# Delta-rule attention, then hash-routed experts, on one core: raw query products copied by ScalarE, the first expert's last rows computed with its early ones, weight loads and banks laid out anew

## The chip, the cores and the metric

One core of a Trainium2 chip runs the kernel in one launch. Its engines are TensorE (PE in the profile; PEld are its weight loads), VectorE (DVE), ScalarE (ACT), GpSimd (POOL) and SyncE (SP), whose queue issues most transfers. Each engine runs its instructions in order and waits on semaphores. The metric is the device time of one execution in microseconds (us). All data are float32.

## The reference

The first half is a delta-rule recurrence over 768 steps, for 4 batches of 8 heads with 48 numbers each; the second sends each of the 3072 resulting rows (384 wide) through one of 8 experts, chosen by a hash of its token number.

```python
for t in range(S):                       # S = 768
    y[:, :, t] = einsum('bhd,bhde->bhe', q_t, state)
    v_old = einsum('bhde,bhd->bhe', state, k_t)
    state = state + b_t * einsum('bhd,bhe->bhde', k_t, v_t - v_old)
...
expert_idx = token_ids * 2654435761 % 8
for e in range(8):
    xe = x[expert_idx == e]
    out[expert_idx == e] = maximum(xe @ w1[e], 0) @ w2[e]   # 384 -> 1024 -> 384
```

Here `k_t` is the normalised key, and `x` the attention's rows in the order of batch and step.

## The kernel before, in words

*Attention.* The 768 steps are 24 chunks of 32 (`c`), in groups of four (`g`). Partitions hold the four batches as quarters of 32. For each group keys and queries are loaded (`load_turn`) and turned by PE transposes and ACT copies into `KQ` (`turn`; L439, L444). Groups 2 and 3 keep theirs in the two `wide` tiles, which later hold the first expert's weights. `gram` (L465) forms products of keys with keys (`GK`, copied by ACT, L475) and of queries with keys (`GQ`). The latter are read from a PSUM bank by DVE and multiplied by a causal mask on the way (L481), with the highest priority. `inverse` (L553 to L596) inverts a 32x32 triangle for each head and chunk of a group by 31 pairs of DVE steps: a product into `tmp` (L596), a sum into `U` (L594). `turn_back` transposes it (L610). ACT spreads the result and the masked products over two halves (`Tz`, `MT`; L522).

`chunk(c)` is the recurrence: PE asks the state for keys and queries (L631), solves with `Tz` (L681), ACT copies `W` (L696), PE updates the state in `psS` (L704), ACT copies the new state (L727), PE adds the part inside the chunk (L744), ACT writes the rows to `x_sb` (L753), and GpSimd scatters them by expert to a buffer in HBM (L759). From chunk 20 on a chunk is split in halves. `scale_v` (L541) prepares V.

*The order.* Every piece of the attention is a `task` with an engine, an estimated time, names it reads and writes, and for PE a count of instruction words. `order` places the tasks on the engines by a list schedule with these estimates and the resulting order is emitted. It also models PE's code: blocks of 256 words, each `FETCH` = 3750 ns after the one before at the earliest. Idle PE time is filled with matmuls on an identity (L1124).

*Banks.* There are eight PSUM banks: two `z`, `psX`, `psY` and four slices of the tile `psS`, which serve as scratch (`homes`) until the first state update claims them.

*First expert.* `first_expert` loads the weights of the expert with rank 0 (`FIRST`) into the `wide` tiles once their keys are used up (L93, L959), in bursts of four transfers. When 18 of the 24 chunks are stored (`SOON`) it fetches 256 of its rows into `xq0` (the buffer's end is padded with zeros from `xq0` before, L969), and computes both layers for them (L995, L1006) after the last chunk. While the last inverse's memory becomes free, the second expert's weights are loaded by `parts`, three transfers at a chunk's store.

*Experts.* After the attention its PSUM pools close and new ones open (`ps_h` with 4 banks, `ps_t` and `ps_o` with 2 each). The loop over `RANKS` starts with `FIRST`, whose last up to 128 rows (the late column) are fetched into `xq_late` and go through `gemm1` (L1158) and `gemm2` (L1174). Each later expert has `gemm1`, whose evictions alternate between ACT (L1161) and DVE (L1163), then `gemm2_turned` (L1195) or `gemm2`. Between the hidden blocks of one expert, `between` loads weights and rows for those that follow and lets DVE turn the next one's rows (`turn`, L107). Rows go out by a GpSimd scatter (L1184). `xqs` are two row buffers, used in turn by rank.

Of the kernel before, what the change touches and what calls it, by code (L numbers as in the profile page):

```python
# [11 lines left out]
F32 = mybir.dt.float32  # L12
# [8 lines left out]
def kernel(  # L21
# [11 lines left out]
    nc = tc.nc  # L33
# [37 lines left out]
    xqs = [keep.tile([P, NBL, QW], F32, name=f"xq{i}") for i in range(2)]  # L71
    xq_late = keep.tile([P, P // C, QW], F32, name="xq_late")

# [67 lines left out]
    idx_i = keep.tile([P, SC], I32)  # L141
    numbers_first = wide[1][:, FO * DIN + SC * DIN:FO * DIN + SC * DIN + SC]
# [12 lines left out]
    with ExitStack() as phase1:  # L155
# [17 lines left out]
        ps = phase1.enter_context(tc.tile_pool(name="ps", bufs=1, space=PSUM))  # L173
# [35 lines left out]
        psS = ps.tile([P, B, BANK], F32, name="psS")  # L209
        homes = zs + [psX, psY] + [psS[:, b] for b in range(B)]  # L210
# [59 lines left out]
        def order():  # L270
# [27 lines left out]
            BLOCK, FETCH = 256, 3750.0  # L298
# [39 lines left out]
            while len(done) < n:  # L338
# [25 lines left out]
                if t["words"]:  # L364

                    for m in range(issued // BLOCK, (issued + t["words"]) // BLOCK + 1):
                        if m == len(begun):
                            if m > 1:
                                have = max(have, begun[-1]) + FETCH
                            begun.append(max(s, have))  # L370
                        s = max(s, begun[m])
# [78 lines left out]
        def gram(c, parts=(0, 1)):  # L450
# [21 lines left out]
            for r in range(2):  # L472
                if 0 in parts:
# [3 lines left out]
                             ACT.Copy), job=(job, r))  # L477
            for r in range(2):
# [165 lines left out]
        def chunk(c):  # L644
# [47 lines left out]
            over = ((len(zs), *range(len(zs) + 2, len(homes))), (1,)) if c == NU - 1 else ((), ())  # L692
            for i, hs in enumerate(hheads if split else (range(0, H),)):
                task("ACT", 300 if split else 390, (xn[i],),
                     (w_names[i],) if split else w_names,
                     lambda i=i, hs=hs: nc.scalar.activation(  # L696
                         W[:, hs.start:hs.stop], pws[i][:, hs.start:hs.stop], ACT.Copy),
                     release=over[i])
            if c < NU - 1:
                S1, K4 = Ss[(c + 1) % 2], K4s[c % 3]  # L700

                def update(us):
                    for u, b in pairs(us):
                        nc.tensor.matmul(  # L704
                            psS[:, b, 2 * D * u:2 * D * u + 2 * D],
# [10 lines left out]
                new = psS[:, :, 0:H * D].rearrange("p b (u r d) -> p b u r d", r=2, d=D)  # L716
                for i in range(2):
                    part = slice(HU // 2 * i, HU // 2 * i + HU // 2)
                    for r in range(2):

                        for q in range(2 if split else 1):
                            bs = slice(2 * q, 2 * q + 2) if split else slice(0, B)

                            def renew(r=r, q=q, bs=bs, part=part):
                                put, get = [t[half(r), bs, part, r] for t in (S1, new)]
# [221 lines left out]
        def first_expert():  # L947

            def weights(i):
                def go():  # L950
                    if not i:
                        which_first.append(expert_at(FIRST, mybir.EngineType.SP))
                        for part in w1_parts(which_first[0], w1_first, nc.sync):
                            part()
                        return
                    src = moe_w2[bass.ds(which_first[0], 1)].rearrange(
                        "o (f p) d -> p (o f) d", p=P)
                    for at in range(0, FO, 2):
                        nc.sync.dma_start(out=w2_first[:, at:at + 2], in_=src[:, at:at + 2])  # L959

                task("SP", 2500, ("lim",), tuple(
                    f"KQ{2 + i}{a}{b}" for a in range(2) for b in range(B)) + (f"w{1 + i}",), go,
                    kb=600)

            which_first = []
            weights(0)
            weights(1)
            rows = x_dram[N:].rearrange("n x -> (n x)").rearrange("(p y) -> p y", p=P)
            task("SP", 500, ("xq0",), ("x_pad",), lambda: nc.sync.dma_start(  # L969
                out=rows, in_=xqs[0].rearrange("p i x -> p (i x)")), kb=700, hold=120000)  # L970

            def early_rows():
                row = value(AT_ROW + E + 1, mybir.EngineType.SP, N)
                got = load_x(row, SC * P // C, xqs[0], nc.sync)
                got.append(load_numbers(row, SC, P, numbers_first[:, :, None], nc.sync))
# [345 lines left out]
```

## Time and profile before

| | |
|---|---|
| time, median of 9 runs | 524.84 us (520.92 to 529.6) |
| profiled execution, its own time | 520.77 us |
| its span | 519.2 us |
| granted PE clock over the span | 0.966 |
| PE busy | 469.7 us (90%), 6652 matmuls |
| DVE busy | 230.9 us (44%) |
| ACT busy | 189.3 us (36%) |
| moved by DMA | 60.61 MB, 117 GB/s over the span |
| DMA queue of instructions (q8) | 53 packets, 0.87 MB |

The span runs from the first to the last instruction that the profile shows; what lies around it, 1.6 us, is in the time of the execution. Shares of busy time are means over stages with different limits: attention fills the first 246 us, the first expert follows up to 279.16 us, and the seven others up to the last matmuls near 508 us. A line of a timeline gives start, duration, engine, line, operation, what it writes and reads, and how many instructions are merged; brackets give idle time of the engine before it and what ended it ("issue" is a wait for nothing that the profile shows).

| stage (us) | PE busy | DVE busy | ACT busy | clock | GB/s |
|---|---|---|---|---|---|
| 39 to 52 | 6.68 | 8.79 | 4.97 | 0.76 | 139 |
| 65 to 78 | 12.09 | 12.11 | 10.79 | 1.00 | 104 |
| 156 to 169 | 10.42 | 8.10 | 8.62 | 0.87 | 121 |
| 221 to 234 | 9.61 | 6.00 | 2.79 | 0.74 | 244 |
| 260 to 273 | 11.56 | 1.83 | 2.47 | 1.00 | 257 |

### The profile page before, as it was taken

What the parts mean: (1) busy time and instruction counts of PE and PEld (TensorE: products, weight loads), DVE (VectorE), ACT (ScalarE), POOL (GpSimd) and SP (SyncE); (2) the same over time, 40 slices, a digit from 0 to 9 for tenths busy, and PEclk for the clock granted to TensorE, in tenths of its full rate; (3) what the DMA queues carried; (4) which work ended last, traced back from release to release, by engine and by line L of the source; (5) the groups of instructions that cost most, each with busy time, mean ns of one, the idle gap of its engine ahead of it and who ended that gap; (6) DMA issues with size and microseconds to landing.
All of it is one profiled execution on the core that took longest, in us unless ns stands there. A gap on an engine that the chain in (4) does not pass through costs nothing. (4 is left out here: it accounts for less than half of the span.)

```text
span 519.2 us, 15841 instructions
## 1 busy us (share of the span) xinstructions
PE 469.7 (90%) x6652; PEld 318.7 (61%) x6652; DVE 230.9 (44%) x736; ACT 189.3 (36%) x415; POOL 70.5 (14%) x106
## 2 busy tenths in 40 slices
PE   8865999999998889879989999999999999999990
PEld 6654667777775667667766555556555565665650
DVE  5796899899896899643011202103012020120100
ACT  4633687888786687523120101101011010110100
POOL 6000011202101121111010001303102012102010
PEclk9977799999998999979999999999999999999997
DMA  9969757674567274591399954544943006401000
GB/s 142 167 101 139 135 103 140 131 136 89 145 138 125 53 202 96 127 242 53 85 257 197 239 113 131 121 91 136 190 144 82 0 24 160 150 0 42 2 29 15
DMA packets 136748, 60.61 MB, mean 117 GB/s; under 512 B 122957, under 2 KB 131265, under 8 KB 136676
## 3 DMA queue, kind: packets, MB, share of 16 engines
q1 hardware_dynamic: 131140, 49.80, 48.0%
q0 software_dynamic: 5344, 9.66, 5.8%
q8 instruction: 53, 0.87, 0.8%
q10 hardware_dynamic: 192, 0.12, 0.1%
q14 instruction: 19, 0.16, 0.1%
HBM read 49.19 MB, written 10.42 MB: 115 GB/s over the span
## 5 line engine op out<-in xcount | busy, mean ns | idle before, releaser
L1158 PE MATMUL h_ps<-xT,w_sb 128*128 128x424 f32 (+3 forms) x336 | 113.4, 491 | 0.0
L1158 PEld LDWEIGHTS h_ps<-xT,w_sb 128*128 128x128 f32 x336 | 62.9, 190 | 43.1 <-issue 14.9
L1163 DVE TENSOR_SCALAR h_sb<-h_ps 128x424 f32<-128x424 f32 (+4 forms) x32 | 17.0, 531 | 138.8 <-PE h_ps L1158 102.9
L1195 PE MATMUL oT_ps<-h_sb,w_sb 128*128 128x424 f32 (+1 forms) x192 | 66.4, 506 | 0.0
L596 DVE TENSOR_TENSOR tmp<-U,Ni 128x112 f32<-128x112 f32 (+15 forms) x186 | 61.6, 338 | 2.8 <-ACT U L580 0.2
L594 DVE TENSOR_TENSOR U<-U,tmp 128x112 f32<-128x112 f32 (+15 forms) x186 | 61.6, 338 | 2.9
L1184 POOL DMA_INDIRECT out_dram<-o_sb,tokens x26 | 30.3, 1167 | 208.0 <-ACT o_sb L1180 163.0
L1195 PEld LDWEIGHTS oT_ps<-h_sb,w_sb 128*128 128x128 f32 x192 | 36.2, 190 | 28.4 <-issue 15.6
L759 POOL DMA_INDIRECT x_scratch<-x_sb,slot x24 | 24.3, 1012 | 206.2 <-ACT MT L522 115.9
L727 ACT ACTIVATE S<-psS 48x384 f32<-48x384 f32 (+1 forms) x92 | 42.7, 464 | 14.3 <-PE psS L704 13.0
L1174 PE MATMUL o_ps<-w_sb,h_sb 128*121 128x384 f32 (+1 forms) x144 | 46.9, 486 | 0.0
L1161 ACT ACTIVATE h_sb<-h_ps 128x424 f32<-128x424 f32 (+4 forms) x32 | 15.0, 469 | 72.5 <-PE h_ps L1158 72.5
L1174 PEld LDWEIGHTS o_ps<-w_sb,h_sb 128*121 128x121 f32 (+1 forms) x144 | 26.6, 185 | 19.4
L744 PEld LDWEIGHTS psY<-W,MT 64*64 64x64 f32 x768 | 25.8, 139 | 14.2 <-issue 12.6
L704 PE MATMUL psS<-W,K 32*128 32x96 f32 x736 | 28.0, 281 | 6.2 <-ACT W L696 5.2
L1180 ACT COPY o_sb<-o_ps 106x384 f32<-106x384 f32 (+4 forms) x15 | 7.2, 479 | 69.5 <-PE o_ps L1174 55.1
L744 PE MATMUL psY<-W,MT 64*64 64x48 f32 x768 | 29.5, 225 | 3.1 <-issue 3.0
L681 PE MATMUL psX<-R,Tz 64*64 64x48 f32 x672 | 27.5, 223 | 3.4 <-issue 2.4
L704 PEld LDWEIGHTS psS<-W,K 32*128 32x128 f32 x736 | 23.7, 186 | 10.4 <-ACT W L696 7.7
L1197 ACT COPY oT<-oT_ps 128x424 f32<-128x424 f32 (+1 forms) x8 | 4.0, 499 | 70.9 <-PE oT_ps L1195 70.9
L681 PEld LDWEIGHTS psX<-R,Tz 64*64 64x64 f32 x672 | 23.4, 136 | 8.2 <-issue 4.7
L522 ACT ACTIVATE Tz<-TU,kmask 128x256 f32<-128x256 f32 x40 | 25.0, 720 | 0.5 <-DVE TU L610 0.5
(192 smaller groups left out, 583.8 us busy)
## 6 DMA issues: line engine op xcount, KB each, us to landing
w_sb<-in_moe_w_dram SPq DMA_DIRECT2D x32, 384.0 KB
w_sb<-in_moe_w_dram SPq DMA_DIRECT2D x6, 1536.0 KB
keys<-in_k_dram SPq DMA_DIRECT2D x24, 192.0 KB
Qt<-in_q_dram SPq DMA_DIRECT2D x24, 192.0 KB
V<-in_v_dram SPq DMA_DIRECT2D x96, 48.0 KB
K<-in_k_dram SPq DMA_DIRECT2D x96, 48.0 KB
wide<-in_moe_w_dram SPq DMA_DIRECT2D x8, 384.0 KB
xq<-x_scratch SPq DMA_DIRECT2D x12, 144.0 KB
```

The source lines that it names most:

```text
L522: lambda e=e: nc.scalar.activation(out[:, :, e].rearrange(order_of), in_.rearrange(order_of), ACT.Copy, scale=kmask[:, e:e + 1]))
L594: nc.vector.tensor_tensor(U[:, n:, 0:n], U[:, n:, 0:n], t, op=ALU.add)
L596: nc.vector.tensor_tensor(t, U[:, j:n, 0:n].to_broadcast([P, m, n]), Ni[:, j, n:, None].to_broadcast([P, m, n]), op=ALU.mult)
L681: nc.tensor.matmul(pws[i][rows, h], lhsT=Tz[rows, h].rearrange("p e i -> p (e i)"), rhs=R[rows, h], start=(h == (hs.start if split else 0) ...
L704: nc.tensor.matmul(psS[:, b, 2 * D * u:2 * D * u + 2 * D], lhsT=K4[quarter(b), u].rearrange("p r d -> p (r d)"), rhs=W[quarter(b), 2 * u:2 ...
L727: copy = nc.scalar.activation(put, get, ACT.Copy)
L744: nc.tensor.matmul(py[rows, h], lhsT=MT[rows, h].rearrange("p e i -> p (e i)"), rhs=W[rows, h], start=(c == 0 and h == 0), stop=True, skip ...
L759: put = nc.gpsimd.indirect_dma_start(out=x_dram[0:N, :], out_offset=bass.IndirectOffsetOnAxis(ap=slot[:, c:c + 1], axis=0), in_=x_sb, in_o ...
L1158: nc.tensor.matmul(h_ps[:, :width], lhsT=w1_sb[:, co, fo * P:(fo + 1) * P], rhs=xT[:, co, :width], start=(co == 0), stop=(co == CO - 1))
L1174: nc.tensor.matmul(o_ps[0:rows], lhsT=h_sb[:, fo, col * rows:(col + 1) * rows], rhs=w2_sb[:, fo, :], start=(fo == 0), stop=(fo == FO - 1))
L1184: scat = nc.gpsimd.indirect_dma_start(out=out[:, :], out_offset=bass.IndirectOffsetOnAxis(ap=idx, axis=0), in_=rows, in_offset=None, bound ...
L1195: nc.tensor.matmul(oT_ps[:, 0:width], lhsT=w2_sb[:, fo, i * P:(i + 1) * P], rhs=h_sb[:, fo, 0:width], start=(fo == 0), stop=(fo == FO - 1))
```

## The change

For chunks 0 to 11 the query products are copied raw from PSUM by ACT, and one DVE multiply in SBUF masks both halves, without the priority. The planner's model of code fetches gets two values, 4600 ns before 58 us and 3800 after. The four banks of `psS` are separate tiles until chunk 0's update, one tile while the state lives there, and separate again after the last `W`; the experts use the same eight banks (`hidden`, `results`) in place of pools of their own. The late column becomes a second set of tasks beside the first expert's early ones, with `xq0` and a new tile `late` as its buffers. The first expert's weights are eight single transfers, each tied in the plan to the store of a chunk from 11 to 18; the zeros are four transfers at chunks 5 to 8. The second expert's weights, the third's and the third's rows are issued after the second's rows, and the loop over experts leaves out `FIRST`. The second row buffer `xq1` lies in memory that opens after the attention.

```diff
-    xqs = [keep.tile([P, NBL, QW], F32, name=f"xq{i}") for i in range(2)]
+    xqs = [keep.tile([P, NBL, QW], F32, name="xq0")]
+    late = keep.tile([P, DIN], F32, name="late")
...
-        psS = ps.tile([P, B, BANK], F32, name="psS")
-        homes = zs + [psX, psY] + [psS[:, b] for b in range(B)]
+        others = ctx.enter_context(ExitStack())
+        homes = zs + [psX, psY]
+        state = []
+        def open_banks(in_one):
+            others.close()
+            pool = others.enter_context(tc.tile_pool(name="others", bufs=1, space=PSUM))
+            if in_one:
+                state[:] = [pool.tile([P, B, BANK], F32, name="psS")]
+            else:
+                homes[4:] = [pool.tile([P, BANK], F32, name=f"bank{i}") for i in range(B)]
+        open_banks(False)
...
-            BLOCK, FETCH = 256, 3750.0
+            BLOCK, FETCH, BUSY_FETCH, BUSY = 256, 3800.0, 4600.0, 58000.0
...
-                                have = max(have, begun[-1]) + FETCH
+                                have = max(have, begun[-1])
+                                have += BUSY_FETCH if have < BUSY else FETCH
...
+            if c < 3 * GC:
+                for r in range(2):
+                    task("ACT", 320, (names[r],), (f"GQ{c % 12}{r}",),
+                         lambda r=r: nc.scalar.activation(GQ[:, :, r], view(r)[:, :, 1],
+                                                          ACT.Copy), job=(job, r))
+                both = (f"GQ{c % 12}0", f"GQ{c % 12}1")
+                task("DVE", 340, both, both, lambda: nc.vector.tensor_tensor(
+                    GQ, GQ, mask[:, None, None, :].to_broadcast([P, HU, 2, C]), op=ALU.mult))
+                return
...
                 def update(us):
+                    if c == 0 and us.start == 0:
+                        open_banks(True)
...
-                task("SP", 2500, ("lim",), tuple(
+                task("SP", 600, ("lim", f"x_dram{11 + 4 * i + j}"), tuple(
                     f"KQ{2 + i}{a}{b}" for a in range(2) for b in range(B)) + (f"w{1 + i}",), go,
-                    kb=600)
+                    kb=380)
...
+            for i in range(4):
+                part = slice(NBL * QW // 4 * i, NBL * QW // 4 * (i + 1))
+                task("SP", 500, ("xq0", f"x_dram{5 + i}"), ("x_pad",), lambda part=part:
+                     nc.sync.dma_start(out=pad[:, part], in_=zeros[:, part]), kb=180)
...
+            columns("late", AT_ROW + E, slice(SC, SC + 1), NU, xq_late, "xq_late", xT_late)
+            for fo in range(FO):
+                job = new_job(1, early=True)
+                for co in range(CO):
+                    task("PE", 240, ("w1", f"xTlate{co}"), (f"j{job}",),
+                         lambda fo=fo, co=co, job=job: nc.tensor.matmul(
+                             bank(job)[:, 0:P], lhsT=w1_first[:, co, fo * P:(fo + 1) * P],
+                             rhs=xT_late[:, co], start=(co == 0), stop=(co == CO - 1)),
+                         words=2, job=(job, 0), idle=True, boost=-1e5)
...
-                if i in stores and parts:
-                    for part in parts[:3]:
-                        part()
-                    parts = parts[3:]
-            for part in parts:
-                part()
-            w_tiles[0] = w1_first, w2_first
...
+        xqs.append(m_q.tile([P, NBL, QW], F32, name="xq1"))
+        def hidden():
+            return homes[next(banks[0]) % 4]
+        def results():
+            return homes[4 + next(banks[1]) % 4]
...
-            fetch(FIRST)
             fetch(RANKS[1])
+            for part in parts:
+                part()
+            w_tiles[2] = load_w(expert_at(RANKS[2], mybir.EngineType.SP), w_pool2, nc.sync)
+            fetch(RANKS[2])
             n_ov = nc.values_load(ov_i[0:1, NOV:NOV + 1], min_val=0, max_val=NOV)
             for c in range(CO):
-                turn(FIRST, c)
+                turn(RANKS[1], c)
             for k in range(SC):
                 send_rows(o_first[:, k], idx_i[:, k:k + 1], True)
+            send_rows(o_late, idx_i[:, SC:SC + 1], True)
             for i, e in enumerate(RANKS):
+                if e == FIRST:
+                    continue
...
-                    to = i + 2 if i < 2 else i + 1
+                    to = max(3, i + 1)
```

`columns` is the fetch of rows, the DVE turns and the token numbers as they were in `first_expert`, for a given set of columns:

```python
def columns(name, at, ks, chunks, xq, xq_name, xT):
    n = ks.stop - ks.start
    task("SP", 2500, ("x_pad", "lim", *(f"x_dram{i}" for i in range(chunks))),
         (xq_name, "numbers" + name),
         lambda: rows_of(at, n, xq, numbers_first[:, ks]), kb=200 * n)
    for c in range(CO):
        task("DVE", 70 + 130 * n, (xq_name,), (f"xT{name}{c}",),
             lambda c=c: turn_x(xq, n * P // C, xT, c))
    task("DVE", 220, ("numbers" + name, "lim"), ("idx" + name,), lambda: number_of(ks))
```

## The prediction

> **What bounds the kernel now.** I read the page's slices first, then the timelines of TensorE (PE), VectorE (DVE) and the SyncE queue (SP). The slices (13 us each) show three stages:
>
> ```profile
> PE   8865999999998889879989999999999999999990
> DVE  5796899899896899643011202103012020120100
> PEclk9977799999998999979999999999999999999997
> ```
>
> The reader is to see that PE is full from the 20th slice on (the experts, from 246 us, at full clock) and has holes before it; that DVE is fullest in slices 3 to 16; and that the granted clock sinks in the 3rd to 5th slice, the 13th and the 18th. The change leaves the matmuls of the seven later experts as they are, so 279.16 us to the end (519.2) is taken as fixed. Three places before that are open.
>
> First, the time before chunk 0. Its solve needs the inverse of group 0, a chain of 62 dependent DVE steps (L594, L596) and a transpose (L610):
>
> ```profile
> 46.57 0.33 DVE L784 TENSOR_TENSOR rt<-rt,rt 128x176 f32<-128x176 f32 x1
> 49.98 0.29 DVE L481 TENSOR_TENSOR GQ<-psS,mask 128x128 f32<-128x128 f32 x1 [3.08 <-ACT GK L475]
> 50.72 0.29 DVE L481 TENSOR_TENSOR GQ<-psS,mask 128x128 f32<-128x128 f32 x1 [0.45 <-ACT GK L475]
> ...
> 52.85 0.36 DVE L594 TENSOR_TENSOR U<-U,tmp 128x207 f32<-128x207 f32 x1
> ...
> 60.50 0.51 DVE L481 TENSOR_TENSOR GQ<-z,mask 128x128 f32<-128x128 f32 x2 [1.33 <-ACT GK L475]
> 60.92 1.24 DVE L610 STREAM_TRANSPOSE TU<-U 128x1024 f32<-128x1024 f32 x1
> ```
>
> Columns: start, duration, engine, line, operation, and in brackets DVE's idle time and who ended it. The steps of U stand still from 46.8 to 52.85 us while DVE, in order, waits for products of queries (L481). Those products are needed by later chunks, not by this inverse. What they in turn waited for is PE's code:
>
> ```profile
> 49.04 0.34 PE L465 MATMUL psS<-wide 48*32 48x64 f32 x6 [4.04 <-issue]
> ...
> 63.57 1.14 PE L681 MATMUL psX<-V,Tz 64*64 64x48 f32 x32 [0.31 <-ACT Tz L522]
> ```
>
> At 49.04 PE had waited 4.04 us for nothing but "issue". Between that stop and the one before it (ended at 31.81) PE ran 383 matmuls and 383 weight loads, 766 instructions, three of the planner's blocks of 256:
>
> ```profile
> 31.00:48.50 17.50, 10.37 (x383) 9.48 (x383) 14.26 (x49) 6.71 (x17) 0.00 (x0) 0.77 0.81 112
> 62.50:161.00 98.50, 90.17 (x2486) 69.84 (x2486) 88.76 (x303) 81.37 (x178) 15.33 (x24) 1.00 0.64 128
> ```
>
> So an "issue" stop is a block of code that is late: three came in 17.2 us, 5.7 us each or less. From chunk 0 to chunk 12 PE takes one block in 5.07 us (4972 instructions in 98.5 us) and has 8.3 us idle.
>
> Second, the bursts of expert weights on SP, with the stops that follow:
>
> ```profile
> 149.03 3.13 SPq L93 DMA_DIRECT2D wide<-in_moe_w_dram  x4
> ...
> 216.47 1.35 SPq L93 DMA_DIRECT2D w_sb<-in_moe_w_dram  x3
> ```
> ```profile
> 161.81 0.30 PE L465 MATMUL z<-KQ 48*32 48x64 f32 x4 [2.58 <-issue]
> ...
> 226.27 1.51 PE L744 MATMUL psY<-W,MT 64*64 64x48 f32 x23 [3.02 <-issue]
> ...
> 265.37 2.20 PE L1006 MATMUL psS<-wide,keys 128*128 128x384 f32 x6 [0.47 <-ACT keys L1000]
> 268.54 5.62 PE L1158 MATMUL h_ps<-xT,wide 128*128 128x128 f32 x48 [0.96 <-ACT wide L1011]
> 274.00 5.33 PE L1174 MATMUL o_ps<-wide,h_sb 128*128 128x384 f32 x16
> 279.16 6.21 PE L1158 MATMUL h_ps<-xT,w_sb 128*128 128x424 f32 x17
> ```
>
> A stop of 2.58 us at 161.81 and one of 3.02 at 226.27 begin 10 and 7 us after bursts of 384 KB pieces (the first line group, from SP's queue; four at 149, eight from 216), and the clock then is 0.83 (161 to 171 us) and 0.84 (225 to 246). The last lines are the third place: the first expert's early columns end with a hole of 0.47, its late column begins after one of 0.96, and the next expert follows at 279.16.
>
> **The change, part by part.**
> *Raw products.* Summing the spells of L481 with their waits on DVE up to 60.92 us (18.6 to 19.24, 20.4 to 22.0, 24.8 to 25.5, 26.8 to 27.2, 33.2 to 35.4, 36.7 to 37.7, 46.8 to 52.85, 59.1 to 60.92): 0.6+1.6+0.7+0.4+2.2+1.0+6.1+1.8 = 14.4 us. In the built order of the changed kernel no L481 stands before the first L610 row; six masks do (the new multiply, 128x256 in SBUF, not shown here; the nearest row is L594 at 128x256, 425 ns): 6 x 0.43 = 2.5. Gain 11.9 at most. At least: 26 issue slots of 0.21 less 2.5, 3.0, if the waits only change place. PE's code is the next limit: before chunk 0's solve it has 2280 instructions instead of 2608 (counted in the built order: 2 for a transpose, 4 for a product), so block 9 is the last it needs; that block came at 49.04 already, and 51.7 us (63.57 less 11.9) is later. The 24 raw copies on ScalarE (ACT; nearest row L475, 411 ns) are 10 us at most; ACT is busy 5.7, 8.6, 4.9 and 5.0 of 13 us in the first four slices and hides them. Two new waits: MT spreads (L522) on ACT wait for DVE's mask, with transposed keys and PE behind them; the masks come early in DVE's order, so I take 0.9 off. I take **-11**.
>
> *Work put after chunk 0.* The built order has 32 transposes (8 groups of 4 at 0.58) and 64 products (60 records in 1.07 us, two records each: 2.3) more between the first solve and the last answer: 4.6 + 2.3 = 6.9 us of PE. Without such work a chunk takes 6.81 us (194.90 to 201.71); chunks 1 to 15 took 122.4, which is 20.2 over 15 x 6.81. Of that 5.5 are issue stops of 0.25 us or more, and 14.7 stand against 60 transposes and 320 products by the same rates, 8.7 + 11.4 = 20.1: 0.73. So 0.73 x 6.9 = **+5.0** (0 if the 8.3 us of holes take it, 6.9 if none).
>
> *Banks reopened at chunk 0.* The update of chunk 0 (L704) now waits until the four banks are read; in ACT's order two spreads (L522 Tz, 720 ns, 0.45 apart) and four raw copies (0.2 apart) stand between W and that: **+1.5** (0 to 2).
>
> *Weights.* The 1.5 MB bursts become eight 384 KB pieces, one a chunk, from chunk 11 to 18, and the second expert's 3.1 MB moves behind its rows, under the first expert. What the bursts cost: two chunks at 162 us took 21.5 against 18.2 by the rates above (6.81 each, 16 transposes 2.3, 64 products 2.3), 3.3; chunk 20 to 21 took 11.15 against 7.3 for the next, 3.9; together 7.2. The pieces still meet the code, so I take **-5** (0 to -7.2). On SP each piece stands ahead of one chunk's loads of K and V (0.45 us of issue; those loads are for two and four chunks later, which hides it). The 700 KB of zeros (134.60) go in four at chunks 5 to 8; no stop followed them, 0.
>
> [...]
>
> *Late column.* The same 32 matmuls, now mixed into the early ones: the two holes go (-1.4), one L995 of 0.43 comes back: **-1**. In the built order its first product stands 18 early and 8 output products behind the last answer, 13 us after it (18 x 0.43 + 8 x 0.65); its rows were turned 8 us after it (254 against 246), so it waits for nothing.
>
> *SP's new order.* Second expert's rows, its weights, the third's weights, the third's rows: 7.5 MB from 253.7. At the 257 GB/s of the slice from 260 that is 29 us: weights of the second by 269, needed at 278; third's rows at about 283. On DVE the turn of those rows (L107) stands after the eviction of the second hidden block, near 282.5, and the odd evictions (L1163) queue behind it; PE needs the first of their banks at 278 + 7 x 2.14 = 293 (evictions 4.27 us apart for two). Cover of 10 us, cost 0; gone, each us of lateness costs one.
>
> Sum: -11 + 5 + 1.5 - 5 - 1 = **-10.5**. The profiled execution took 520.77 (span 519.2 and 1.6 around it), so 510.3. It lies 4.1 under the median of the runs shown (524.84); against that median the forecast is **514**.
>
> **Rivals.**
> *No gain in sum* (the change doesn't do what it says). The planner puts masks and copies where its model has a block in 3.8 or 4.6 us; if blocks come at up to 5.7, DVE stands at masks as it stood at L481. With the least gain, -3 + 5 + 1.5 - 5 - 1 = -2.5: 522.3. For it: DVE still waits in order. Against: the masks wait on ACT alone, and six waits replace 26.
> *Slower: every piece meets a block.* Eight pieces instead of three bursts, while PE needs a block in 5.07 us. Without the burst term the sum is -5.5; if each piece costs 2.58, the smallest of the two stops, 20.6 less the 7.2 that go = +13.4, so +7.9: 532.7. It decides from (7.2 + 5.5 + 2.6)/8 = 1.9 us a piece. For it: the code's share is as tight as said. Against: the 1.5 MB issued from 185.40 to 188.94 caused no stop over 1 us.
> *More gain.* The holes take the moved work and the bursts' cost goes whole: -11 + 0 + 0 - 7.2 - 1 = -19.2: 505.6.
>
> **How the numbers follow.** Forecast 0.66, more gain 0.14, no gain 0.11, every piece 0.09. The range, 503 to 524, holds the first two with the bounds (-11.9 - 7.2 - 1.4 = -20.5, 504.3) and most of the third; above it lies the last rival. 0.5% (2.6 us) is about what a measurement here tells from no change: of the no-gain case 0.02 falls to faster and 0.01 to slower: faster 0.82, same 0.08, slower 0.10.
>
> **What would show it.** In the new profile: the first L610 transpose near 50 us and chunk 0's solve near 52; no DVE wait over 1 us at the masks; chunk 0 to chunk 4 about 3 us longer than the 29.9 of before; no issue stop over 2 us between chunk 11 and the end of attention, with a clock near 1.0 there; from the last answer to the second expert's first matmul 32 us (33.1 before). I am wrong if chunk 0's solve is after 58 us, if weights still stop PE, or if PE stands still in the second expert.

## The result and the profile after

The changed kernel takes 509.12 us (median of 20 runs, 504.5 to 516.35) beside 523.73 for the kernel before (62 runs): ratio 0.973, 95% interval 0.971 to 0.975. Ratios here and below leave out executions more than 1.5% above the fastest of their kernel, so they differ a little from the quotients of the medians. The forecast was 514 us with a range of 503 to 524. The profiled execution after took 509.12 us with a span of 507.5, where the one before took 520.77 with 519.2: 11.65 us less, where the prediction's sum said 10.5.

The page's slices of the changed kernel (12.7 us each):

```profile
PE   8974999999799798999999999999999999999990
DVE  5799899998897888571200203013021021110100
PEclk9977899999999999799999999999999999999996
```

From the 17th slice to the last but one PE shows nothing below 9; before, the last 8 stood in the 21st (which the prediction's "full from the 20th slice on" passed over). The granted clock still sinks at the start and once more, in the 17th slice; the sinks of the 13th and the 18th are gone.

VectorE's timeline of the changed kernel ahead of chunk 0 (start, duration, engine, line, operation; L503 is the new mask, L622 and L624 are the old L594 and L596, L638 the old L610):

```profile
41.68 0.37 DVE L624 TENSOR_TENSOR tmp<-U,Ni 128x207 f32<-128x207 f32 x1
41.97 0.42 DVE L503 TENSOR_TENSOR GQ<-GQ,mask 128x256 f32<-128x256 f32 x1
42.31 0.37 DVE L622 TENSOR_TENSOR U<-U,tmp 128x207 f32<-128x207 f32 x1
...
48.53 0.30 DVE L624 TENSOR_TENSOR tmp<-U,Ni 128x135 f32<-128x135 f32 x1
48.74 1.24 DVE L638 STREAM_TRANSPOSE TU<-U 128x1024 f32<-128x1024 f32 x1
```

TensorE's timeline just after it, with the idle time before a row and who ended it in brackets (L709 is the solve, L1192 a fill that keeps PE busy, L690 puts the next chunk's V into its bank, L779 is the answer, L738 the update):

```profile
51.32 1.94 PE L709 MATMUL psX<-V,Tz 64*64 64x48 f32 x32 [5.59 <-ACT Tz L550]
53.19 2.06 PE L1192 MATMUL psY<-ident 128*128 128x512 f32 x2
55.05 0.84 PE L690 MATMUL psX<-V,minus 128*128 128x384 f32 x2
55.82 1.14 PE L779 MATMUL psY<-W,MT 64*64 64x48 f32 x32
56.89 1.15 PE L738 MATMUL psS<-W,K 32*128 32x96 f32 x32
```

The mask stands in the chain of U like any other step, with no wait of its own, and the transpose comes at 48.74 us instead of 60.92. Chunk 0's solve follows at 51.32, 12.25 us earlier. But PE had then been idle for 5.59 us, the solve takes 1.94 us instead of 1.14 (the granted clock is 0.50 from 46 to 54 us), and the update of the state comes 5.57 us after the solve instead of 2.15.

From such rows the two profiled executions can be laid side by side, place by place:

| us | before | after | difference | the terms that met there |
|---|---|---|---|---|
| start to chunk 0's solve | 63.57 | 51.32 | -12.25 | raw products -11 |
| solve to update of chunk 0 | 2.15 | 5.57 | +3.42 | banks +1.5 |
| update of chunk 0 to that of 4 | 29.92 | 30.08 | +0.16 | moved work +3 (of the 5) |
| 4 to 12 | 66.41 | 66.82 | +0.41 | moved work, weights |
| 12 to 20 | 58.78 | 62.16 | +3.38 | moved work, weights |
| 20 to the last answer's end | 25.25 | 19.39 | -5.86 | weights |
| to the second expert's first matmul | 33.08 | 31.24 | -1.84 | late column -1 |
| to the end | 240.04 | 240.92 | +0.88 | SP's order 0 |

Between solve and last answer the sum is +1.51, and the prediction's three terms there gave 5 + 1.5 - 5 = 1.5. So the account by places came out nearly as forecast. Whether each gain belongs to the part of the change that was named for it is another question, and such a table can't answer it. The experiments answer it for most parts, and the answer is different.

### The profile page after: what moved, and what is told of

Its sections match the earlier page's. It is cut to its first block, busy times and chain, and to the rows that moved or that the text cites. A ratio compares the mean times of both kernels' runs of the same rounds, so it can differ in the third digit from the quotient of the medians.

```text
span 507.5 us, 15828 instructions
## 1 busy us (share of the span) xinstructions
PE 466.4 (92%) x6648; PEld 317.4 (63%) x6648; DVE 229.9 (45%) x720; ACT 191.9 (38%) x443; POOL 71.2 (14%) x106
## 5 line engine op out<-in xcount | busy, mean ns | idle before, releaser
L1263 PE MATMUL bank<-h_sb,w_sb 128*128 128x424 f32 (+1 forms) x192 | 66.4, 506 | 0.0
L624 DVE TENSOR_TENSOR tmp<-U,Ni 128x87 f32<-128x87 f32 (+15 forms) x186 | 62.3, 340 | 3.6 <-ACT U L608 0.3
L622 DVE TENSOR_TENSOR U<-U,tmp 128x87 f32<-128x87 f32 (+15 forms) x186 | 62.0, 338 | 2.9
L1226 PE MATMUL z<-xT,w_sb 128*128 128x424 f32 (+3 forms) x168 | 57.4, 491 | 0.0
L1263 PEld LDWEIGHTS bank<-h_sb,w_sb 128*128 128x128 f32 x192 | 36.2, 190 | 28.4 <-issue 15.6
L1231 DVE TENSOR_SCALAR h_sb<-z 128x424 f32<-128x424 f32 (+3 forms) x14 | 7.9, 562 | 89.5 <-PE z L1226 89.5
L1242 PE MATMUL bank<-w_sb,h_sb 128*121 128x384 f32 (+1 forms) x144 | 46.9, 486 | 0.0
L1226 PEld LDWEIGHTS z<-xT,w_sb 128*128 128x128 f32 x168 | 31.6, 190 | 22.2 <-issue 7.6
L1242 PEld LDWEIGHTS bank<-w_sb,h_sb 128*121 128x121 f32 (+1 forms) x144 | 26.6, 185 | 19.4
L779 PEld LDWEIGHTS psY<-W,MT 64*64 64x64 f32 x768 | 25.7, 138 | 10.3 <-issue 8.6
L1226 PE MATMUL psY<-xT,w_sb 128*128 128x424 f32 (+3 forms) x84 | 30.0, 493 | 0.5 <-DVE h_sb L1231 0.5
L738 PE MATMUL psS<-W,K 32*128 32x96 f32 x736 | 27.1, 282 | 3.1 <-ACT W L723 2.9
L1226 PE MATMUL psX<-xT,w_sb 128*128 128x424 f32 (+3 forms) x84 | 29.9, 492 | 0.0
L779 PE MATMUL psY<-W,MT 64*64 64x48 f32 x768 | 29.3, 224 | 0.2
L709 PE MATMUL psX<-R,Tz 64*64 64x48 f32 x672 | 26.6, 221 | 2.9 <-issue 2.9
L709 PEld LDWEIGHTS psX<-R,Tz 64*64 64x64 f32 x672 | 22.8, 134 | 7.3 <-issue 5.1
L738 PEld LDWEIGHTS psS<-W,K 32*128 32x128 f32 x736 | 23.1, 187 | 6.2 <-ACT W L723 4.5
```

Source lines behind the costliest of these rows:

```text
L622: nc.vector.tensor_tensor(U[:, n:, 0:n], U[:, n:, 0:n], t, op=ALU.add)
L624: nc.vector.tensor_tensor(t, U[:, j:n, 0:n].to_broadcast([P, m, n]), Ni[:, j, n:, None].to_broadcast([P, m, n]), op=ALU.mult)
L709: nc.tensor.matmul(pws[i][rows, h], lhsT=Tz[rows, h].rearrange("p e i -> p (e i)"), rhs=R[rows, h], start=(h == (hs.start if split else 0) ...
L738: nc.tensor.matmul(state[0][:, b, 2 * D * u:2 * D * u + 2 * D], lhsT=K4[quarter(b), u].rearrange("p r d -> p (r d)"), rhs=W[quarter(b), 2 ...
L779: nc.tensor.matmul(py[rows, h], lhsT=MT[rows, h].rearrange("p e i -> p (e i)"), rhs=W[rows, h], start=(c == 0 and h == 0), stop=True, skip ...
L1226: nc.tensor.matmul(h_ps[:, :width], lhsT=w1_sb[:, co, fo * P:(fo + 1) * P], rhs=xT[:, co, :width], start=(co == 0), stop=(co == CO - 1))
```

## The experiments

All runs are given as a ratio to the kernel before on the same chip, for the chips differ: the kernel before took 524.34, 514.42 and 517.83 us (medians) in the three groups of runs. The first group holds raw products alone, the first run without raw products and both on weight loads; the second both on fetch times, raw copies first and late column last; the third the rest. The changed kernel's own 0.9731 comes from other executions, and its profile has the pace of the first group's chip (see the end). No run of it is on record for the chips of the other two groups, so a comparison with it there is one across chips.

### Raw products alone

In the kernel before, the raw copies and masks for chunks 0 to 11 were put ahead of the old masked reads, with the lines of the change, and nothing else:

```diff
+            if c < 3 * GC:
...
+                both = (f"GQ{c % 12}0", f"GQ{c % 12}1")
...
+                return
             for r in range(2):
                 if 1 in parts:
```

> The kernel before, with the raw ScalarE copies and the masks in SBUF for chunks 0 to 11 and nothing else of the change. My sum: chunk 0's solve falls from 63.57 to about 52 us (-11); the work that then comes after chunk 0 gives 5 us back and the opening of the banks 1.5, so the time is about 4.5 us below the kernel before, ratio 0.991. Rival 'the lead stays': nothing is given back, about -11, ratio 0.979. Rival 'the planner needs the rest too': DVE still waits, solve after 58, ratio 1.00 or above.

Ratio 1.0055 (1.0011 to 1.0099): about 2.9 us slower than before. The solve came at 58.07, 5.5 us earlier than before but just past the bound of 58. So the third case came, and the profile shows its reason: VectorE still waits. TensorE, ScalarE and VectorE in this kernel (L465 makes the products, L475 copies those of keys, L590 copies a diagonal for VectorE's inverse, L606 is the old L596):

```profile
50.24 0.35 PE L465 MATMUL z<-wide 48*32 48x64 f32 x6 [3.97 <-issue]
```
```profile
50.98 0.60 ACT L475 ACTIVATE GK<-psS 128x128 f32<-128x128 f32 x2 [4.09 <-PE psS L465]
...
52.24 0.25 ACT L590 ACTIVATE U<-d 128x32 f32<-128x32 f32 x1
```
```profile
52.52 0.38 DVE L606 TENSOR_TENSOR tmp<-U,Ni 128x31 f32<-128x31 f32 x2 [3.59 <-ACT U L590]
```

ScalarE's copy for VectorE stood behind copies of products that TensorE hadn't made yet. (In the changed kernel that copy comes at 45.21, ahead of them, and VectorE doesn't wait for it.) TensorE's waits for VectorE's masks from 8 to 64 us, 5.5 us in the kernel before, became 3.9 us of waits for ScalarE's raw copies. The wait moved on by one engine. A lead of 5.5 us that isn't in the time has been paid for elsewhere; see the account below.

### The change without raw products, twice

The same tasks taken out of the changed kernel, so that DVE reads PSUM with the mask and the highest priority again; run once in the first group and once in the last.

> The changed kernel with the query products of the first 12 chunks again read from PSUM and masked by DVE. My sum: 4.5 us slower than the changed kernel (about 513.6 at its 509.1; ratio to the kernel before about 0.98), chunk 0's solve at 60 us or later. Rival 'the lead stays': 11 us slower than the changed kernel, ratio to before 0.994. Rival 'weights and tail do it all': within 1.5 us of the changed kernel, ratio 0.973 to 0.976.

> The changed kernel without the raw products once more, on another chip than the first time (ratio 0.9652 to the kernel before there, the changed kernel 0.9731). Theory 'raw products cost in sum': 0.962 to 0.969 again. Rival 'chance of six executions': 0.971 to 0.976.

Ratios 0.9652 (0.9595 to 0.9709) and 0.9674 (0.9633 to 0.9716), where the changed kernel has 0.9731 (0.9709 to 0.9754). Without the raw products the change is some 3 to 4 us faster. None of the first expectation's cases foresaw that, and the second run bore it out. Chunk 0's solve was at 55.37 and 55.34 us, so 8.2 of its 12.25 us of lead over 63.57 are there without the raw products.

### Both weight loads back as bursts, and no pieces at all

In the first kernel the pieces of the first expert's weights wait for nothing but their tile, and the second expert's are issued at the stores as before; the other leaves the eight pieces out, so its first expert multiplies whatever its tiles hold.

```diff
-                task("SP", 600, ("lim", f"x_dram{11 + 4 * i + j}"), tuple(
+                task("SP", 600, ("lim",), tuple(
...
+                if i in stores and parts:
+                    for part in parts[:3]:
+                        part()
+                    parts = parts[3:]
```

> The changed kernel with both weight loads as bursts inside the attention again (first expert's as soon as its tile is free, second expert's at the stores after the last inverse); the instructions of TensorE, VectorE and ScalarE stand in the order of the changed kernel. My term: 5 us slower than the changed kernel, with an issue stop over 2 us and a chunk 20 to last answer of 23 us or more (19.4 in the changed kernel). Rival 'the stops belong to the code, not to the bursts': within 1.5 us of the changed kernel. Rival 'all of it': 7 us or more slower.

> The changed kernel without the eight 384 KB loads of the first expert's weights at all: the first expert multiplies what its tiles hold, the rest is computed as before. My term: the pieces still cost 2.2 us (7.2 less 5), so 2.2 us faster than the changed kernel, with a clock near 1 from 195 to 208 us. Rival 'pieces cost nothing': within 1 us. Rival 'every piece meets a block': 8 us or more faster.

With bursts 0.9843 (0.9788 to 0.9898), 0.0112 or 5.9 us above the changed kernel; without pieces 0.9696 (0.9652 to 0.9740), 1.8 us below it. Both are the sizes of my term (5 and 2.2), though by the ends of the intervals the first may be 1.8 to 9.9 and the second anything from 5.3 faster to 1.6 slower. The signs in the bursts' profile were weaker than expected: chunk 20 to the last answer 21.82 us, and no stop above 1.49. That execution took 509.65 us, the lowest of the six, so the profile shows a mild one. Without pieces the clock is 1.00 from 195 to 208 us, as expected.

### The planner's fetch times, each way

Old and new fetch times exchanged: the new ones alone in the kernel before, the old one in the changed kernel.

```diff
-            BLOCK, FETCH = 256, 3750.0
+            BLOCK, FETCH, BUSY_FETCH, BUSY = 256, 3800.0, 4600.0, 58000.0
```

> The kernel before with the planner's new fetch times (4.6 us a block up to 58 us, 3.8 after) and nothing else of the change. The runs so far put chunk 0's solve at 58.07 us with raw products alone and at 55.37 with all but them (63.57 before, 51.32 with all). Theory 'the order made by the fetch times frees DVE's chain': solve near 55, no issue stop of 4 us before it, time 6 to 8 us below the kernel before (ratio 0.985 to 0.989). Rival 'it was another part (banks apart, order of SP)': solve at 61 or later, ratio 0.997 to 1.003.

> The changed kernel with the old fetch time, 3.75 us for every block, in the planner. Theory 'the fetch times free the chain': solve near 58 as with raw products alone, 6.7 later than in the changed kernel; in the built order the update of chunk 0 follows its solve at once, which gives 3.4 back: 3 to 4 us slower than the changed kernel. Rival 'raw products free it, whatever the planner believes': solve at 53 or earlier, as fast as the changed kernel or faster.

Alone 1.0139 (1.0071 to 1.0207), 7 us slower, with the solve at 66.07. My theory of that moment, that the fetch times free DVE's chain, fell, and its rival (0.997 to 1.003) had the place of the solve right but not the time. The changed kernel with the old time came to 0.9899 (0.9797 to 1.0001), some 9 us worse than with the new ones, by a wide interval, though its solve lay at 53.92, near the rival's bound. But the fallen theory left a clue. The kernel with the fetch times alone and the one without raw products have the same matmuls in the same order through the whole attention, and their solves lie at 66.07 and 55.37 us (one execution each, on two chips). What delays one of them isn't a matmul more.

### Banks apart alone, and back in one tile

What differs are the tiles: in the kernel before, four of the scratch banks are slices of one tile, `psS`; in the changed one each is a tile until chunk 0's update. So this alone was put into the kernel before, and this alone taken from the changed kernel. In both cases every engine keeps its attention instructions in their order; only waits change.

```diff
-        psS = ps.tile([P, B, BANK], F32, name="psS")
-        homes = zs + [psX, psY] + [psS[:, b] for b in range(B)]
+        homes = zs + [psX, psY]
+                homes[4:] = [pool.tile([P, BANK], F32, name=f"bank{i}") for i in range(B)]
```

> The kernel before with the four banks of the state as four tiles until chunk 0's update, where one tile of four banks is opened; every engine has the instructions of the kernel before in the same order, only waits differ. Theory 'one tile makes a write to one of its banks wait for readers of the other three': the waits of TensorE at psS for ScalarE's and VectorE's reads go, chunk 0's solve falls from 63.57 to 58 or less, ratio 0.983 to 0.990. Rival, my prediction's step 'banks reopened at chunk 0': nothing is freed and up to 2 us are added, ratio 1.000 to 1.004.

> The changed kernel with the four banks as one tile again from the start to the end of attention; every engine has the instructions of the changed kernel in the same order, only waits differ. Theory 'one tile': chunk 0's solve at 57 or later (51.32 in the changed kernel), 6 us or more slower, ratio 0.985 or above. Rival 'banks reopened only cost': as fast as the changed kernel or 1.5 us faster, ratio 0.970 to 0.973.

Apart: 0.9897 (0.9863 to 0.9931), 5.4 us faster than before, with the solve at 58.78 (58 or less was expected). In one tile: 0.9767 (0.9714 to 0.9820), with the solve at 58.62 instead of 51.32, as expected; but in time 1.9 us worse than the changed kernel, where 6 were expected, and the interval doesn't tell 1.9 from nothing. So the gain in time is shown in the kernel before; inside the changed kernel only the earlier solve is. The profiled execution with banks apart took 517.04 us, the longest of its six.

TensorE's waits from 8 to 64 us in the kernel before: tile and line that waited, the engine, tile and line waited for, us in total, how often, and the longest.

```profile
PE psS L465 <- issue: 5.6, 2, 4.0
PE psS L465 <- DVE GQ L481: 2.3, 1, 2.3
...
PE psS L465 <- ACT wide L444: 1.1, 3, 0.6
PE psS L465 <- DVE rt L784: 0.9, 1, 0.9
PE psS L819 <- DVE GQ L481: 0.4, 1, 0.4
PE psS L439 <- DVE GQ L481: 0.4, 1, 0.4
...
PE psS L439 <- ACT KQ L444: 0.3, 1, 0.3
```

The same with banks apart alone, where L477 and L456 are the old L465 and L444:

```profile
PE bank L477 <- issue: 6.6, 3, 3.6
...
PE bank L477 <- ACT KQ L456: 0.2, 1, 0.2
```

Six kinds of wait at a slice of `psS` for VectorE or ScalarE, 5.4 us of PE (2.3 + 1.1 + 0.9 + 0.4 + 0.4 + 0.3), shrink to 0.2 at `bank`. A product that goes to one slice waited for the readers of another, because the four slices were followed as one tile. The waits by issue don't go: 5.6 us at `psS` before, 6.6 at `bank`, and over all tiles 5.8 and 8.6, which takes back part of the gain.

### Raw copies first, late column last, and neither raw products nor fetch times

ScalarE's raw copies with the priority that VectorE's masked reads had; the late column's matmuls behind all early ones; and the changed kernel without raw products and with the old fetch time, which leaves banks apart, weights in pieces, late column and SP's order.

```diff
-                                                          ACT.Copy), job=(job, r))
+                                                          ACT.Copy), boost=1e6, job=(job, r))
...
-                         words=2, job=(job, 0), idle=True, boost=-1e5)
+                         words=2, job=(job, 0), idle=True, boost=-2e5)
...
-            BLOCK, FETCH, BUSY_FETCH, BUSY = 256, 3800.0, 4600.0, 58000.0
+            BLOCK, FETCH, BUSY_FETCH, BUSY = 256, 3750.0, 3750.0, 58000.0
```

> The changed kernel with the raw copies of ScalarE put ahead of all else on it (the priority that VectorE's masked reads have); in the built order chunk 0's update then follows its solve, as before the change. Theory 'raw copies late on ScalarE hold the four banks that the update needs': solve to update 2.2 to 2.5 us instead of 5.57, 3 us faster than the changed kernel. Rival 'only a change of place': solve later by as much or chunk 0 to 4 longer by as much, within 1.5 us of the changed kernel.

> The changed kernel with the late column's matmuls after all of the early columns'; the order up to the last answer is unchanged. My term for mixing it in was 1: last answer to the second expert's first matmul 32.3 us or more (31.24 in the changed kernel), 1 us slower. Rival 'mixing costs nothing, PE is full in either order': 31.2, within 0.5 us.

> The changed kernel without the raw products and with the old fetch time of 3.75 us: banks apart, weights in pieces, late column and SP's order alone. Theory 'banks, weights and tail are the gain': ratio 0.962 to 0.970, as the changed kernel without raw products (0.9652) or within 2 us of it. Rival 'the fetch times are needed': 4 us or more slower than that, ratio 0.973 or above.

*Raw copies first:* 0.9842 (0.9746 to 0.9937), not 3 us faster but rather slower. Solve to update fell to 3.87 us, not to 2.2, and PE was idle for 7.59 us before the solve. The theory of the late raw copies isn't borne out as a gain. *Late column last:* 0.9749 (0.9692 to 0.9806), 0.9 us above the changed kernel by the middle, and 31.79 us instead of 31.24 from the last answer to the second expert. That lies between the two cases, and the interval can't tell. Of the 0.55 us 0.40 is a wait for the second expert's weights, so 0.15 is left for the order, nearer to the rival. *Neither:* 0.9711 (0.9679 to 0.9743), between the two cases and the changed kernel's time again (0.9731). Banks, weights and tail make all of the gain; raw products and fetch times together add nothing to it that these runs can tell. Against the kernel without raw products alone (0.9652 and 0.9674) the fetch times are worth 2 to 3 us here, by intervals that overlap.

### An account of TensorE's time

Why does a solve that comes 5.5 us earlier bring nothing? TensorE's windows of 2 us say where the time went: for each the busy time, the rest of the window as idle, and the busy time times one less the granted clock as lost to half clock. What remains is work at full clock. Summed up to chunk 0's solve and from there to the last answer (us):

| kernel | solve at | work | idle | half clock | then: work | idle | half clock |
|---|---|---|---|---|---|---|---|
| before | 63.57 | 41.7 | 16.2 | 5.7 | 158.4 | 19.8 | 4.3 |
| raw products alone | 58.07 | 36.0 | 15.8 | 6.3 | 159.2 | 22.0 | 10.1 |
| fetch times alone | 66.07 | 39.8 | 16.6 | 9.7 | 156.2 | 15.9 | 7.8 |
| changed, one tile | 58.62 | 34.8 | 16.9 | 6.9 | 159.4 | 11.2 | 6.5 |
| banks apart alone | 58.78 | 40.5 | 12.2 | 6.1 | 151.7 | 15.3 | 18.4 |
| neither raw nor fetch | 58.97 | 42.1 | 12.5 | 4.4 | 154.7 | 12.4 | 1.6 |
| without raw products | 55.37 | 39.3 | 11.9 | 4.2 | 162.5 | 11.2 | 1.7 |
| changed | 51.32 | 35.0 | 13.4 | 2.9 | 163.8 | 15.0 | 5.3 |

The four kernels whose scratch banks are one tile (the upper half) are idle for 15.8 to 16.9 us before the solve, the four with banks apart for 11.9 to 13.4. Of the other six with banks apart five lie between 12.3 and 13.8; raw copies first has 15.2, half of it the wait of 7.59. Raw products don't lower that number. Their lead of 5.5 us is 5.7 us less work ahead of the solve (1158 matmuls, fills among them, instead of 1305). Yet the work behind the solve grew by only 0.8 us. The lead went into idle time there (22.0 for 19.8) and half clock (10.1 for 4.3). In the changed kernel, beside the one without raw products, it is the same: 4.3 us less work ahead, 1.3 more behind, 3.8 more idle and 3.6 more half clock. (Work after the solve isn't quite comparable across chips, for the reason given at the end.) One profiled execution stands behind each row, so a difference of a few us in half clock is no property of a kernel.

The clocks of all the executions behind the ratios point the same way. The mean granted clock is 0.948 with raw products alone and 0.956 before, 0.968 in the changed kernel and 0.978 without raw products, 0.961 with bursts, 0.952 with the fetch times alone and 0.968 before on that chip. A clock lower by 0.008 over 520 us is 4 us, an estimate of the most it can cost. With banks apart alone it is 0.951, and 0.953 before: banks apart save waits and no clock. Why the orders with raw products get a lower clock wasn't found.

## Why the prediction came out, point by point

**The time was right, and two of its terms were not.** The sum was 1.2 us from the profiled difference, and the mechanism that carried the largest part of it was not the one that I named. That the sum held is luck: raw products were forecast at -6 and cost 3 to 4, banks were forecast at +1.5 and bring 5.4 measured alone, and the two errors largely cancel. The planner's fetch times had no term at all; they cost 7 us alone, and in the changed kernel save 2 to 3 without raw products and some 9 with them, the last by a wide interval. And a range from 503 to 524 had room for most of the rival without a gain.

- *Raw products, -11 (with +5 for work put after chunk 0: -6).* The place was right: solve at 51.32 for 52, masks without waits. The cause was wrong. "The steps of U stand still from 46.8 to 52.85 us while DVE, in order, waits for products of queries" is what the profile shows, but taking DVE's waits as what the raw copies remove failed. I had written that those products waited for PE's code. The queue of instructions (q8) does start a packet between 46 and 47 us, within the stop that ended at 49.04, and three from 31.81 to 49.04, where PE ran 766 instructions. But the products also waited for PE, which waited at a shared tile. Taking DVE out of the queue leaves PE's idle time as it was, 15.8 us for 16.2. Measured alone the term is +2.9 us, not -6, and in the changed kernel it still costs 3 to 4. The rival "no gain in sum" had the better number for this one part. Its reason, VectorE standing at the masks, is seen for 2.2 us with raw products alone and not in the changed kernel.
- *Work put after chunk 0, +5.* 32 transposes and 64 products were counted right. In the account the work ahead of the solve fell by 41.7 - 35.0 = 6.7 us, for my 6.9. But for chunks 0 to 4 I expected +3, and only 0.16 came, though 16 of the transposes and 48 of the products do stand there: from chunk 0's update to chunk 4's TensorE's busy time grew from 27.07 to 28.55 us and its idle time fell from 2.85 to 1.53. There the holes took the work; my 0.73 was too high. Between chunks 12 and 20, where 8 transposes and 32 products more stand, 3.38 us were lost.
- *Banks reopened at chunk 0, +1.5 (0 to 2).* This is the step that failed with its sign. I priced the wait that the new tile brings and not the waits that the old one had made. The kernel without raw products reopens its banks too and goes from solve to update in 2.21 us, against 2.15 before, so the opening costs nothing there; banks apart alone bring -5.4 us (-7.2 to -3.6). The 3.42 us that the changed kernel loses at this place are gone when the raw products are left out.
- *Weights, -5 (0 to -7.2).* Borne out: 5.9 us when both bursts come back, and 1.8 more to be had when the pieces go (2.2 expected). Between chunk 11 and the last answer no stop by issue was above 0.88 us, where two of 2.58 and 3.02 had been. The clock didn't stay near 1 throughout, as the next section shows. The rival "every piece meets a block" fell: it asked for over 1.9 us a piece, and all eight cost 1.8, at most 5.3 by the intervals.
- *Late column, -1.* 1.84 less in the profile, of which mixing it in is 0.15 to 0.55 by its own run on another chip. The rest isn't separated.
- *SP's new order, 0.* The profile has 0.9 us more there, 0.52 of it by something that the step left out. The third expert's rows go into `xq0`, where the late column's hidden values (`h_late`) now lie until its last product.

SyncE's longest wait from 240 to 280 us in the changed kernel (L100 fetches rows, L1075 is that product), and its timeline when the wait ends:

```profile
SPq L100 <- PE bank L1075: 5.9, 1, 5.9
```
```profile
266.77 7.30 SPq L100 DMA_DIRECT2D xq<-x_scratch  x4
```

VectorE's timeline, where L108 turns those rows and L1231 evicts:

```profile
281.02 0.65 DVE L108 STREAM_TRANSPOSE xT<-xq 128x448 f32<-128x448 f32 x1 [9.30 <-DMA xq<-x_scratch]
281.59 0.56 DVE L1231 TENSOR_SCALAR h_sb<-psY 128x424 f32<-128x424 f32 x1
```

TensorE's timeline of the same stretch, from the last L1075 to the hole in the second expert:

```profile
265.93 0.81 PE L1075 MATMUL bank<-wide,xq 128*128 128x384 f32 x2
266.58 4.43 PE L1226 MATMUL z<-xT,w_sb 128*128 128x424 f32 x12
...
282.20 2.40 PE L1226 MATMUL psY<-xT,w_sb 128*128 128x424 f32 x6 [0.52 <-DVE h_sb L1231]
```

The queue waited 5.9 us for L1075; the rows were turned at 281.02, 14.4 us after the second expert began at 266.58, where I had 5 (283 for 278). The evictions behind the turn were late by so much that PE stood still for 0.52 us, which the prediction had named as a sign of being wrong. Holding `h_late` elsewhere wasn't tried.

## What to carry to other kernels

When an engine waits, ask what the one before it in the chain waits for, down to the last; here a fix at the first link moved the wait (5.5 us for VectorE became 3.9 for ScalarE). Scratch banks that were slices of one tile were followed as one here (5.4 us of PE's waits, 0.2 with banks apart): before the cost of splitting or joining tiles is priced, compare the waits of both kernels at that tile. And a milestone that comes earlier proves no gain (a solve 5.5 us earlier came with a time 2.9 us longer): count how much work was moved behind it, and compare what remains of idle time and low clock.

## What the runs showed of the hardware

**A stop of 3.02 us was followed by half clock.** Windows of the kernel before around its stop of 3.02 us: length, then busy time and instructions of PE, its weight loads, DVE, ACT and POOL, granted clock, share of DMA time, GB/s.

```profile
223.00:226.00 3.00, 0.24 (x9) 0.18 (x6) 1.49 (x5) 1.30 (x4) 0.00 (x0) 0.79 1.21 185
226.00:229.00 3.00, 2.73 (x57) 2.64 (x60) 0.98 (x2) 0.49 (x1) 0.00 (x0) 0.50 1.00 301
229.00:232.00 3.00, 3.00 (x75) 2.67 (x67) 0.98 (x3) 0.33 (x1) 1.20 (x2) 0.58 1.20 223
232.00:235.00 3.00, 2.63 (x65) 2.23 (x64) 1.26 (x2) 0.58 (x2) 0.00 (x0) 1.00 0.81 246
```

The same of the changed kernel at the sink of the 17th slice:

```profile
198.00:201.00 3.00, 1.73 (x56) 1.38 (x44) 2.73 (x9) 1.07 (x3) 1.19 (x2) 1.00 0.82 211
201.00:204.00 3.00, 2.81 (x34) 1.71 (x34) 1.04 (x4) 1.32 (x4) 0.00 (x0) 0.65 0.11 22
204.00:207.00 3.00, 3.00 (x60) 2.77 (x63) 2.58 (x7) 1.24 (x3) 0.00 (x0) 0.50 0.30 52
207.00:210.00 3.00, 2.87 (x80) 2.47 (x71) 1.90 (x4) 0.57 (x2) 1.98 (x2) 0.72 0.11 39
```

Where PE did 0.24 us of work in 3, the clock then is 0.50 and 0.58, and it is 1.00 again after 232 us; 2.73 x 0.50 + 3.00 x 0.42 = 2.6 us of work at full clock are lost there, an estimate. In the changed kernel PE is busy for 1.73 of 3 us, no stop is longer than 0.88, and still the clock falls to 0.50 for some 7 us. In the profile with banks apart alone a stop of 2.20 us was followed by 19 us at half clock (158 to 177) with TensorE busy throughout, and this isn't explained. In the windows of 2 and 3 us of all these kernels the clock is never above 1.00 nor below 0.50; the 0.72 of 207 to 210 us above is 0.50 in its first microsecond, 0.65 in its second and 1.00 in its third. Among executions of one kernel the time goes with the mean clock: before, on the first chip, from 518.9 us at 0.964 to 527.8 at 0.939.

**The same program has another pace on another chip.** The kernel without raw products ran on two. TensorE's timeline of one chunk that has nothing but the recurrence, from one update (L728) to the next, on the first chip:

```profile
191.49 1.15 PE L728 MATMUL psS<-W,K 32*128 32x96 f32 x32 [0.58 <-ACT W L713]
...
195.34 0.87 PE L649 MATMUL psY<-S,KQ 128*32 128x96 f32 x32
196.14 1.02 PE L699 MATMUL psX<-R,Tz 64*64 64x48 f32 x28
197.37 0.35 PE L699 MATMUL psX<-R,Tz 64*64 64x48 f32 x4 [0.21 <-issue]
198.29 1.15 PE L728 MATMUL psS<-W,K 32*128 32x96 f32 x32 [0.58 <-ACT W L713]
```

On the second:

```profile
192.93 1.15 PE L728 MATMUL psS<-W,K 32*128 32x96 f32 x32 [0.59 <-ACT W L713]
...
196.78 0.87 PE L649 MATMUL psY<-S,KQ 128*32 128x96 f32 x32
197.57 1.14 PE L699 MATMUL psX<-R,Tz 64*64 64x48 f32 x32
199.30 1.15 PE L728 MATMUL psS<-W,K 32*128 32x96 f32 x32 [0.59 <-ACT W L713]
```

On the first the solve (L699) breaks off before its last matmuls (0.21 by issue, and a later start of the rest), and the next update comes after 6.80 us (198.29 less 191.49); on the second the solve is whole and the chunk takes 6.37. The other rows shown last equally long. It isn't one execution's chance: between the updates of chunks 15 and 19 the shortest step from one update to the next takes 6.8 us in this profile and in those of the kernels before and after, and 6.37 on the second chip with one tile and with neither raw products nor fetch times as well. TensorE waits by issue at the solve 10 times in the kernel before (2.4 us), at the pace of the first chip, and never in the kernel without raw products on the second; 10 x 0.43 is 4.3 us, an estimate, beside 6.5 and 9.9 us between the chips' medians of the kernel before (524.34, 517.83 and 514.42). What sets that pause wasn't found.
